# A new order for all engines in a fused attention and PReLU kernel, with alpha loaded in 16 rows

## The chip, the cores and the metric

One core of a Trainium2 chip runs the whole kernel. The metric is the device time of one execution in microseconds. A median over runs is compared, and one further execution was profiled.

## The reference

Eight batches, eight heads, 512 tokens and 32 states of width 64. Tokens attend to the states and the states to the tokens; both results, side by side, are the rows of a two-layer network.

```python
scores = scale * x @ state.T                  # per batch and head
a = softmax(scores);  xread = a @ state       # 512 rows of 64
a2 = softmax(scale * state @ x.T)
sread = a2 @ x                                # 32 rows of 64
rows = concat(xread, sread) over heads        # 8 * 544 = 4352 rows of 512
h = rows @ w_in                               # 512 -> 2048
g = maximum(h, 0) + alpha * minimum(h, 0)     # alpha: one value per column of h
out = g @ w_out                               # 2048 -> 512
```

## The kernel before

The kernel never forms xread. It multiplies the states with w_in first (`m`, 32 states of 4 heads in one PSUM bank, one `m` for each batch and each quarter f of w_in) and then the softmax weights with that product, so the first layer of a batch is 16 pairs of products (`F.b.jc`, two of 128x512). `f` is one half of such a pair, used for the first three of batch 0, where the weights of the first four heads are there before those of the others.

All work is one list of steps, `ORDER`, from which each engine gets its instructions in that order; there is no scheduler behind it, and waits come from the data and from the PSUM banks alone. A step's last numbers name the PSUM bank (0 to 5) or the engine: a is ScalarE (ACT), v is VectorE (DVE), p is GpSimd (POOL). A seventh place, the tile `two`, is shared by the scores of all batches and by those `m` that name no bank. The steps are:

- `lx0`, `lx`, `lst`, `wi`, `wo`: loads by GpSimd's DMA queue, which turns float32 into float16 on the way: x of a batch (batch 0 in two halves), the states, a quarter of w_in, a quarter of w_out.
- `stc`, `stt`, `sto`, `str`, `sro`: the states cast, transposed on TensorE and copied out.
- `xt`, `xo`: x of batches 0 and 1, transposed on TensorE and copied out. From batch 2 on, `xd` does it by a transposing DMA in SyncE's queue.
- `sc`: scores. `sb`, `smax`, `ssh`, `sexp`, `ssum`, `snorm`, `wb`: the softmax over the states (a 32x32 block transpose on VectorE, the maximum, the shift and the scaling on GpSimd, the exponential on ScalarE, and the transpose back). For batch 0 it is done in two halves, `.0` and `.1`; the state softmax of batch 0 reads `sc.0.0` and `sc.0.1`, the token softmax a second computation `sc.0`.
- `tm`, `te`, `tsum`, `tn`, `tt`, `rd`, `rdo`: the softmax over the tokens and the read of x with it.
- `m`, `mo`: states times w_in and its eviction, in two halves 0 and 1.
- `N`, `G`: on ScalarE `neg = relu(-h)`; on VectorE `g = neg * (1 - alpha) + h`. `oma` computes 1 - alpha.
- `S.b.q.jc2`, `O`: second layer, two products of 128x512 of the eight pairs that a block of 128 rows needs; then the eviction and store. `S` with jc2 of 6 and 7 reads the last quarter of w_out.
- `R`, `RO`, `L`, `LO`: the second layer of the 32-state rows, and the last block of rows in three pieces.
- `Z.k.n`: n products of zeros into bank k, whose results nobody reads.

Alpha (2048 values) is loaded by ScalarE's queue straight into the layout that `G` wants, value 128 jc + p in partition p, which makes each value a run of 4 bytes:

```python
alpha_sb = consts.tile([128, n_jc], F32)
nc.scalar.dma_start(alpha_sb, moe_alpha.rearrange("(jc p) -> p jc", p=128))
```

The order begins with the first batch's loads on GpSimd, then 20 zero products, the first states, 18 zero products, and the first two transposes of x:

```
stc lx0.0 lx0.1 oma id Z.1.20 stt.0 Z.2.18 xt.0.0.0.1 sto.a xt.0.1.0.2 xo.0.0.0.v lst xo.0.1.0.v
```

`xt.b.j.g` takes token half j of head group g; both transposes named here read the first half of batch 0's x, and `sc.0.0` needs both.

Of the kernel before, what the change touches and what calls it, by code (L numbers as in the profile page):

```python
# [28 lines left out]
N.0.9 G.0.6 S.0.1.2 smax.1 te.1.1 te.1.0 F.0.11.4 G.0.9 ssh.p.1 F.0.8.3 wo.3 N.0.8 N.0.11 S.0.0.3
S.0.1.3 m.0.3 G.0.8 F.0.10.0 mo.0.3.a.0 N.0.10 sexp.1 S.0.2.3 mo.0.3.v.1 xd.2 G.0.11 G.0.10  # L30
S.0.3.0.3 m.1.3 S.0.3.1 mo.1.3.a.0 F.0.14.4 S.0.2.4 F.0.13.0 N.0.14 tt.0 ssum.1 S.0.0.4 S.0.1.4
S.0.0.5 S.0.3.2 G.0.14 F.0.12.4 N.0.13 G.0.13 F.0.15.0 snorm.p.1 N.0.12 N.0.15 mo.1.3.a.1 wb.1
S.0.3.3 S.0.1.5 S.0.3.4 G.0.12 S.0.2.5 G.0.15 S.0.3.5 F.1.2.4 S.0.2.6 N.1.2 F.1.0.0 tsum.1 S.0.2.7
N.1.0 S.0.1.6 S.0.1.7 G.1.2 O.0.2.a sc.2 m.2.1.4.5 S.0.0.6 O.0.1.a F.1.7.2 mo.2.1.a.0 mo.2.1.a.1
G.1.0 F.1.1.0 tm.2 sb.2 F.1.3.4 N.1.7 S.0.0.7 S.0.3.6 N.1.1 G.1.1 N.1.3 tn.1.0 O.0.0.a te.2.0
F.1.5.5 S.0.3.7 N.1.5 G.1.3 F.1.9.0 S.1.1.0.1 G.1.7 F.1.4.4 smax.2 O.0.3.a S.1.1.1 tn.1.1 G.1.5
rd.0.2 te.2.1 N.1.9 G.1.9 m.2.3 F.1.6.3 N.1.4 rdo.0.a F.1.12.5 N.1.6 lx.3 G.1.4 F.1.13.2 N.1.12
F.1.8.0 G.1.6 G.1.12 S.1.2.0.4 N.1.13 G.1.13 ssh.p.2 N.1.8 S.1.1.2 F.1.11.3 G.1.8 F.1.10.5 N.1.11
S.1.2.1 N.1.10 G.1.11 G.1.10 S.1.2.2 sexp.2 S.1.1.3 ssum.2 F.1.14.2 F.1.15.0 snorm.p.2 mo.2.3.a.0
S.1.1.4 mo.2.3.a.1 S.1.1.5 m.3.2 m.4.2.3.5 N.1.14 tt.1 tsum.2 N.1.15 G.1.14 mo.3.2.a.1 S.1.1.6  # L40
S.1.2.3 S.1.2.4 mo.3.2.a.0 mo.4.2.a.0 G.1.15 mo.4.2.a.1 S.1.2.5 S.1.1.7 xd.3 O.1.1.a m.3.1.2.0
m.2.2.3.5 sc.3 wb.2 tn.2.1 S.1.2.6 S.1.2.7 mo.3.1.a.1 F.2.15.1 S.1.0.0.0 mo.2.2.a.0 mo.3.1.a.0
O.1.2.a lx.4 mo.2.2.a.1 sb.3 N.2.15 S.1.0.1 tm.3 F.2.13.3 N.2.13 G.2.15 S.1.0.2 F.2.4.2 tn.2.0
F.2.2.4 G.2.13 smax.3 N.2.4 F.2.9.5 F.2.0.1 N.2.9 S.1.0.3 S.1.0.4 G.2.9 S.1.0.5 N.2.2 N.2.0 te.3.0
F.2.12.3 S.1.0.6 N.2.12 G.2.2 G.2.4 G.2.0 xd.4 F.2.7.5 G.2.12 S.1.3.0.4 ssh.p.3 sexp.3 N.2.7 ssum.3
S.1.0.7 te.3.1 F.2.3.2 S.1.3.1 F.2.1.1 N.2.3 S.1.3.2 N.2.1 F.2.8.3 G.2.3 S.1.3.3 G.2.1 S.1.3.4
S.1.3.5 N.2.8 S.1.3.6 G.2.7 F.2.6.2 O.1.0.a N.2.6 m.3.3.1.0 G.2.8 sc.4 rd.1.5 snorm.p.3 F.2.5.3
G.2.6 mo.3.3.a.0 F.2.14.1 rdo.1.a wb.3 N.2.5 tsum.3 S.2.1.0.2 F.2.11.5 mo.3.3.a.1 G.2.5 S.1.3.7
N.2.14 F.2.10.0 F.3.4.3 G.2.14 N.2.11 S.2.1.1 F.3.1.1 lx.5 O.1.3.v N.3.4 S.2.1.2 N.2.10 G.2.11 tt.2
S.2.0.0.4 S.2.1.3 S.2.0.1 G.2.10 F.3.14.5 F.3.9.0 S.2.1.4 tn.3.1 N.3.1 N.3.9 G.3.1 S.2.1.5 S.2.0.2  # L50
G.3.4 tn.3.0 N.3.14 tm.4 F.3.3.1 F.3.8.3 G.3.14 N.3.8 G.3.9 S.2.1.6 S.2.1.7 S.2.0.3 S.2.3.0.5 N.3.3
xd.5 O.2.1.a tt.3 sb.4 G.3.8 smax.4 F.3.6.0 F.3.2.2 te.4.0 S.2.3.1 S.2.3.2 N.3.6 N.3.2 F.3.13.3
S.2.0.4 te.4.1 ssh.p.4 N.3.13 G.3.3 G.3.6 S.2.0.5 F.3.7.1 G.3.2 S.2.0.6 N.3.7 S.2.0.7 sexp.4 G.3.13
G.3.7 S.2.3.3 S.2.3.4 S.2.3.5 m.6.0 O.2.0.v m.5.1.0.2 mo.6.0.a.1 mo.5.1.a.1 rd.3.3 mo.6.0.v.0
rdo.3.a mo.5.1.v.0 rd.2.1 m.4.1.4.2 ssum.4 sc.5 m.4.3.0.3 rdo.2.a S.2.3.6 mo.4.1.a.1 mo.4.1.a.0 tm.5
tsum.4 snorm.p.4 F.3.5.1 mo.4.3.a.0 mo.4.3.a.1 F.3.0.2 F.3.10.4 N.3.0 S.2.3.7 O.2.3.a S.2.2.0.0
S.2.2.1 F.3.11.3 G.3.0 wb.4 S.2.2.2 S.3.3.0.5 F.3.15.2 S.3.3.1 N.3.5 lx.6 G.3.5 te.5.0 te.5.1 N.3.10
N.3.15 S.2.2.3 F.3.12.1 S.2.2.4 N.3.11 S.3.3.2 lx.7 N.3.12 G.3.10 G.3.15 F.4.6.4 N.4.6 tn.4.0
F.4.5.2 G.3.11 F.4.3.3 N.4.5 S.2.2.5 G.3.12 G.4.5 S.3.3.3 F.4.4.1 S.3.3.4 F.4.7.2 N.4.4 S.3.3.5
S.2.2.6 N.4.3 sb.5 N.4.7 S.3.3.6 S.2.2.7 G.4.4 G.4.7 S.3.3.7 F.4.1.1 F.4.0.2 xd.6 O.2.2.a S.3.1.0.0  # L60
O.3.3.a S.3.1.1 F.4.9.5 N.4.1 smax.5 G.4.6 N.4.0 S.3.0.0.4 tn.4.1 S.3.0.1 G.4.1 G.4.0 F.4.8.1
S.3.1.2 tsum.5 N.4.9 ssh.p.5 G.4.3 sexp.5 N.4.8 G.4.9 F.4.11.2 F.4.2.3 N.4.2 S.3.0.2 ssum.5 S.3.0.3
S.3.0.4 tt.4 N.4.11 S.3.1.3 G.4.8 S.3.1.4 S.3.1.5 G.4.2 S.3.1.6 snorm.p.5 m.5.0.5.1 G.4.11 sc.6
m.5.3.3.2 xd.7 wb.5 mo.5.0.a.1 sb.6 S.3.1.7 mo.5.3.a.0 mo.5.0.a.0 F.4.13.1 N.4.13 S.3.0.5 mo.5.3.a.1
S.3.2.0.3 tm.6 S.3.0.6 te.6.0 F.4.10.5 F.5.3.2 smax.6 S.3.2.1 N.4.10 N.5.3 S.3.2.2 S.3.2.3 S.3.0.7
S.3.2.4 S.3.2.5 S.3.2.6 ssh.p.6 G.4.13 O.3.1.a tn.5.0 F.4.14.1 te.6.1 O.3.0.v S.3.2.7 G.4.10 G.5.3
N.4.14 F.4.12.0 G.4.14 O.3.2.a sexp.6 tn.5.1 S.4.1.0.4 m.6.3 m.7.2.5.2 m.5.2.3.1 mo.6.3.v.0 S.4.1.1
mo.5.2.v.0 mo.7.2.a.0 S.4.1.2 mo.5.2.a.1 F.5.15.5 mo.6.3.v.1 mo.7.2.a.1 tt.5 S.4.1.3 N.5.15 G.5.15
F.4.15.3 F.5.12.1 S.4.1.4 F.5.5.2 N.4.12 F.5.13.5 S.4.1.5 N.5.12 N.4.15 G.4.12 tsum.6 G.4.15
S.4.0.0.0 S.4.1.6 S.4.1.7 N.5.5 S.4.0.1 S.4.2.0.3 O.4.1.v G.5.5 S.4.0.2 F.5.10.4 N.5.13 F.5.1.2  # L70
S.4.2.1 G.5.12 F.5.0.1 N.5.10 S.4.0.3 S.4.2.2 S.4.0.4 G.5.13 tn.6.1 N.5.0 G.5.10 N.5.1 G.5.1
m.6.1.5.4 m.7.0 mo.6.1.a.1 mo.6.1.a.0 S.4.0.5 mo.7.0.v.0 S.4.0.6 F.5.2.2 N.5.2 S.4.0.7 mo.7.0.v.1
G.5.0 O.4.0.a rd.4.4 rd.5.5 G.5.2 m.7.3.1.0 rdo.4.a m.6.2.2.4 sc.7 rdo.5.a ssum.6 mo.7.3.a.0
mo.6.2.a.0 snorm.p.6 tn.6.0 S.4.3.0.5 S.4.3.1 mo.7.3.v.1 F.5.11.1 S.4.3.2 sb.7 S.4.3.3 N.5.11 G.5.11
F.5.6.2 F.5.9.0 S.4.2.3 S.4.2.4 F.5.7.1 S.4.3.4 mo.6.2.a.1 F.5.8.4 smax.7 S.4.3.5 S.4.3.6 wb.6
S.4.3.7 S.4.2.5 N.5.9 N.5.8 N.5.7 G.5.9 O.4.3.a G.5.8 F.5.4.0 N.5.4 tt.6 S.5.0.0.4 S.5.2.0.5 S.4.2.6
G.5.7 G.5.4 F.5.14.1 S.5.2.1 tm.7 S.5.0.1 N.5.6 S.4.2.7 F.6.3.0 N.5.14 G.5.6 S.5.2.2 S.5.0.2 te.7.1
F.6.15.2 N.6.3 G.6.3 S.5.2.3 N.6.15 S.5.2.4 S.5.0.3 G.6.15 ssh.p.7 S.5.2.5 F.6.7.0 S.5.1.0.2 N.6.7
S.5.0.4 G.5.14 O.4.2.v S.5.1.1 F.6.6.1 G.6.7 F.6.8.3 te.7.0 S.5.1.2 N.6.6 S.5.1.3 sexp.7 F.6.1.0
tsum.7 N.6.8 N.6.1 G.6.6 S.5.2.6 F.6.0.1 S.5.0.5 tn.7.1 tn.7.0 S.5.0.6 G.6.8 S.5.2.7 F.6.10.3 tt.7  # L80
N.6.0 S.5.1.4 G.6.1 S.5.1.5 S.5.1.6 S.5.1.7 F.6.14.0 N.6.10 O.5.1.a ssum.7 G.6.10 S.5.0.7 F.6.5.3
snorm.p.7 F.6.2.2 N.6.14 N.6.5 G.6.0 S.5.3.0.1 O.5.0.v G.6.14 m.7.1 G.6.5 rd.7.4 rd.6.0 rdo.7.v
N.6.2 O.5.2.a F.6.13.3 S.5.3.1 mo.7.1.v.0 rdo.6.a S.5.3.2 S.5.3.3 mo.7.1.v.1 F.6.9.5 F.8.4.4 N.6.9
G.6.2 S.5.3.4 wb.7 F.6.12.0 G.6.9 F.6.4.2 N.6.13 N.6.12 S.5.3.5 G.6.12 N.6.4 S.5.3.6 S.5.3.7
S.6.0.0.5 S.6.0.1 N.8.4 F.6.11.0 G.6.13 G.6.4 F.8.10.3 N.6.11 S.6.0.2 N.8.10 O.5.3.v G.8.4 S.6.1.0.2
F.7.0.1 S.6.0.3 F.7.7.4 N.7.0 S.6.1.1 G.6.11 S.6.0.4 N.7.7 S.6.0.5 G.7.0 S.6.1.2 F.8.14.0 S.6.1.3
S.6.1.4 G.8.10 S.6.0.6 N.8.14 F.7.3.1 S.6.0.7 G.7.7 S.6.1.5 F.8.3.3 F.7.6.4 G.8.14 N.7.3 F.8.2.0
O.6.0.v G.7.3 F.7.2.5 F.8.9.1 S.6.1.6 N.8.3 G.8.3 S.6.2.0.3 N.8.2 N.7.2 S.6.2.1 G.8.2 S.6.2.2 N.7.6
# [547 lines left out]
```

## Time and profile before

| | |
|---|---|
| median of 3 runs | 218.97 us (218.73 to 219.55) |
| the profiled execution: time, span | 219.66 us, 217.9 us |
| TensorE busy in the span | 210.6 us (97%) |
| VectorE, ScalarE, GpSimd busy | 165.2, 137.4, 71.0 us |
| DMA | 23.12 MB, mean 106 GB/s |

Times in the profile's rows count from the span's start. A timeline row gives the start, the length, the engine (PE is TensorE, DVE VectorE, ACT ScalarE, POOL GpSimd, SP SyncE), the line, the operation, the output and the inputs by the program's names, and how many instructions are merged in it; in brackets stands how long the engine was idle before and what ended that. Products overlap in TensorE, so a merged row is longer than the distance to the next by the tail of its last product.

### The profile page before, as it was taken

How to read it: one execution, taken by the hardware profiler on the slowest of the kernel's cores; microseconds unless marked ns; L12 is line 12 of the kernel's file. 1: busy time of each engine (PE TensorE's matmuls, PEld its weight loads, DVE VectorE, ACT ScalarE, POOL GpSimd, SP SyncE). 2: the span in 40 equal slices, each digit the busy share in tenths (PEclk: the TensorE clock that was granted, in tenths of full speed). 3: DMA queues.
4: the chain of work that ended last, by engine and by line, in shares of the span. 5: the costliest groups of instructions: out<-in, count | busy, mean ns of one | idle time of the engine just before them, and what ended most of it. 6: DMA issues, size and time to landing. Idle time of an engine off the chain costs nothing.

```text
span 217.9 us, 4311 instructions
## 1 busy us (share of the span) xinstructions
PE 210.6 (97%) x1698; PEld 104.2 (48%) x1698; DVE 165.2 (76%) x250; ACT 137.4 (63%) x271; POOL 71.0 (33%) x58
## 2 busy tenths in 40 slices
...
GB/s 69 188 199 206 200 171 117 206 196 113 92 143 100 92 245 101 51 88 187 249 55 99 96 48 53 0 99 48 50 148 3 46 48 51 48 33 15 51 96 144
DMA packets 41748, 23.12 MB, mean 106 GB/s; under 512 B 24192, under 2 KB 38016, under 8 KB 41728
## 3 DMA queue, kind: packets, MB, share of 16 engines
...
q10 hardware_dynamic: 2064, 0.01, 0.5%
...
q14 instruction: 7, 0.06, 0.1%
...
## 4 chain that ended last, share of the span: by engine, by line
PE 84%; DMA 9%; DVE 3%; POOL 1%; issue 1%; ACT 0%; POOLq 0%
PE o L526 47%; PE h L474 23%; DMA xT<-xg 4%; DMA w_in_sb<-in_moe_w_in_dram 3%; PE m_ps L441 3%; PE h L483 3%; PE o L574 3%; DMA xg<-in_x_dram 2%; PE o L546 2%; PE sr_ps L416 2%; PE sc L291 1%; POOL an L352 1%; DVE ts L326 1%; DVE m L463 1%; DVE mx L332 1%
## 5 line engine op out<-in xcount | busy, mean ns | idle before, releaser
L526 PE MATMUL o<-w_out_sb,gt 128*128 128x512 f16 x496 | 125.3, 379 | 0.9 <-DMA w_out_sb<-in_moe_w_out_dram 0.9
L506 ACT ACTIVATE neg<-h 128x512 f32<-128x512 f32 (+1 forms) x144 | 77.1, 579 | 47.8 <-PE h L474 38.4
L514 DVE SCALAR_TENSOR_TENSOR gt<-neg,oma_sb,h 128x512 f16<-128x512 f32 x128 | 89.9, 738 | 16.5 <-ACT neg L506 15.6
L526 PEld LDWEIGHTS <-gt 128*128 128x128 f16 x496 | 47.3, 98 | 56.4 <-issue 4.5
L474 PE MATMUL h<-aT,m 128*128 128x512 f16 x250 | 68.3, 379 | 0.0
L474 PEld LDWEIGHTS <-m 128*128 128x128 f16 x250 | 24.1, 98 | 28.4 <-issue 0.6
L397 POOL TENSOR_SCALAR e<-e,r 128x512 f16<-128x512 f16 x16 | 25.0, 1566 | 20.4 <-DVE r L393 16.6
L463 ACT CAST m<-m_ps 128x512 f16<-128x512 f32 x50 | 27.1, 606 | 4.6 <-PE m_ps L441 4.3
L352 POOL TENSOR_TENSOR an<-ts,r 128x1024 f16<-128x1024 f32 (+1 forms) x9 | 15.4, 1719 | 33.2 <-DVE r L349 14.8
L338 POOL TENSOR_TENSOR ts<-ts,mx 128x1024 f32<-128x1024 f32 (+1 forms) x9 | 15.5, 1720 | 30.9 <-DVE mx L332 30.9
L564 ACT COPY osb<-o 128x512 f32<-128x512 f32 x22 | 12.9, 591 | 14.9 <-PE o L526 14.9
L441 PE MATMUL m_ps<-w_in_sb,stT 64*32 64x512 f16 x256 | 11.3, 383 | 0.6 <-DMA w_in_sb<-in_moe_w_in_dram 0.4
L383 ACT ACTIVATE e<-sc,nb 128x512 f16<-128x512 f32 x16 | 11.1, 700 | 1.1 <-DVE nb L375 1.1
L360 DVE STREAM_TRANSPOSE aT<-an 128x1024 f16<-128x1024 f16 (+1 forms) x9 | 10.1, 1120 | 1.9 <-POOL an L352 1.9
L514 DVE SCALAR_TENSOR_TENSOR gs<-neg,oma_sb,h 128x256 f16<-128x256 f32 x16 | 7.5, 476 | 4.5 <-ACT neg L506 4.5
L463 DVE CAST m<-m_ps 128x512 f16<-128x512 f32 x14 | 9.1, 679 | 2.0 <-ACT m L463 1.6
L372 DVE TENSOR_REDUCE nb<-sc 128x2 f32<-128x1024 f32 x8 | 9.6, 1202 | 0.5 <-PE sc L291 0.5
L332 DVE TENSOR_REDUCE mx<-ts 128x32 f32<-128x1024 f32 (+1 forms) x9 | 9.8, 1091 | 0.0
L348 DVE TENSOR_REDUCE r<-ts 128x32 f32<-128x1024 f32 (+1 forms) x9 | 9.8, 1087 | 0.0
L483 PE MATMUL h<-XS,w_in_sb 128*128 128x256 f16 x64 | 9.4, 273 | 0.0
L584 DVE COPY osr<-o 128x512 f32<-128x512 f32 x1 | 0.7, 692 | 11.3 <-PE o L574 11.3
L344 ACT ACTIVATE ts<-ts 128x1024 f32<-128x1024 f32 (+1 forms) x9 | 8.6, 960 | 0.2 <-POOL ts L338 0.2
...
## 6 DMA issues: line engine op xcount, KB each, us to landing
...
```

Source lines behind the costliest of these rows:

```text
L332: nc.vector.tensor_reduce(cols(live["mx", b], j, S // N), blocks(cols(live["ts", b], j, S)), AX.X, ALU.max)
L338: engine(e).tensor_tensor(ts, ts, over_blocks(cols(live["mx", b], j, S // N)), ALU.subtract)
L352: engine(e).tensor_tensor(blocks(cols(live["an", b], j, S)), blocks(cols(live["ts", b], j, S)), over_blocks(cols(live["r1", b], j, S // N) ...
L397: nc.gpsimd.tensor_scalar_mul(e2, e2, live["r2", b][:, g : g + 1])
L441: nc.tensor.matmul(t[N * k : N * (k + 1), :], st_head(b, h)[64 * r : 64 * r + 64, :], w_in_sb[64 * r : 64 * r + 64, c, 512 * f : 512 * (f ...
L463: copier(e)(m_tile(b)[:, f, g, :], live["mp", b, f][g])
L474: nc.tensor.matmul(h.rearrange("p (r j s) -> p r j s", r=2, j=2), ms[b][:, f, g, 128 * j : 128 * (j + 1)], weights(b, g), start=(g == 0), ...
L483: nc.tensor.matmul(h, w_in_sb[:, c, 128 * jc : 128 * (jc + 1)], XS[:, c].rearrange("p q n b -> p (q n b)"), start=(c == 0), stop=(c == n_c ...
L506: nc.scalar.activation(neg, h, RELU, bias=0.0, scale=-1.0)
L514: nc.vector.scalar_tensor_tensor(gt, negs.pop((b, jc)), oma_sb[:, jc : jc + 1], h, ALU.mult, ALU.add)
L526: nc.tensor.matmul(outs[b, q], gts[b, jc][:, 128 * q : 128 * (q + 1)], w_out_sb[:, jc, :], start=(jc == 0), stop=(jc == n_jc - 1),)
L564: copier(e)(osb, t)
```

## The change

`ORDER` is written anew. The last 166 of its 1055 steps keep their order, apart from PSUM banks; before them the steps are the same in kind and nearly in number, but stand in other places, and some evictions go from ScalarE to VectorE or back. The state shift of batch 7 and the scaling of batch 4 go from GpSimd to VectorE. The zero products are 74 in place of 82. The first eight of GpSimd's loads now stand ahead of its first softmax step: the first quarter of w_out and the third of w_in are moved there. The last quarter of w_out stands ahead of the state shift of batch 1.

Alpha is loaded as 16 rows of 128 values, into 16 of 32 partitions that are set to zero first, and VectorE transposes four 32x32 blocks before it computes 1 - alpha.

```diff
-stc lx0.0 lx0.1 oma id Z.1.20 stt.0 Z.2.18 xt.0.0.0.1 sto.a xt.0.1.0.2 xo.0.0.0.v lst xo.0.1.0.v
-Z.0.6 sc.0.0 xt.0.1.1.3 xt.0.0.1.4 sb.0.0 xo.0.0.1.v smax.0.0 xo.0.1.1.a str.0.5 sc.0.1 str.1.0 wi.0
-sro.0.a lx.1 wi.1 ssh.p.0.0 sb.0.1 Z.1.3 sc.0 Z.5.7 m.0.0.1.2 sro.1.a sexp.0.0 smax.0.1 m.3.0.3.4
-ssh.p.0.1 tm.0 mo.0.0.a.1 sexp.0.1 ssum.0.0 m.1.0.5.0 ssum.0.1 te.0.1 te.0.0 mo.1.0.v.1 wo.0
-mo.1.0.a.0 snorm.p.0.0 mo.3.0.a.1 Z.2.28 xt.1.1.1.2 xt.1.1.0.5 mo.0.0.a.0 snorm.p.0.1 wb.0.0
-mo.3.0.a.0 m.2.0 xt.1.0.1.0 xo.1.1.0.v xt.1.0.0.4 f.0.0.0.1 f.0.1.0.5 wi.2 mo.2.0.a.0 wb.0.1
-mo.2.0.a.1 f.0.1.1 xo.1.0.0.v N.0.1 m.0.1.3.4 f.0.0.1 mo.0.1.a.1 m.1.1 xo.1.1.1.v N.0.0 xo.1.0.1.v
-mo.0.1.v.0 f.0.2.0.2 F.0.3.0 f.0.2.1 F.0.4.3 mo.1.1.v.0 mo.1.1.a.1 F.0.7.4 G.0.1 N.0.2 G.0.0 wo.1
-F.0.5.5 N.0.3 G.0.2 wi.3 m.4.0 N.0.4 S.0.0.0.1 N.0.5 G.0.3 tsum.0 S.0.1.0.2 N.0.7 mo.4.0.a.1 G.0.4
...
+lx0.0 lx0.1 stc id Z.1.20 stt.0 lst wi.0 sto.v xt.0.1.0.1 Z.0.18 xt.0.0.0.2 xo.0.1.0.v xo.0.0.0.v
+Z.0.6 sc.0.0 xt.0.0.1.3 oma xo.0.0.1.a lx.1 wi.1 wo.0 sb.0.0 xt.0.1.1.4 xo.0.1.1.v str.0.5 sc.0.1
+sro.0.a smax.0.0 sb.0.1 str.1.0 smax.0.1 wi.2 sro.1.a ssh.p.0.0 Z.1.3 sc.0 ssh.p.0.1 Z.5.3 m.0.0.1.2
+tm.0 sexp.0.0 m.1.0.3.4 mo.0.0.a.0 ssum.0.0 sexp.0.1 m.2.0.5.0 ssum.0.1 mo.1.0.v.1 te.0.0 Z.1.24
+xt.1.1.1.1 mo.2.0.a.1 mo.2.0.a.0 xt.1.0.1.0 snorm.p.0.0 xt.1.0.0.5 wb.0.0 mo.0.0.a.1 snorm.p.0.1
+mo.1.0.a.0 xt.1.1.0.4 xo.1.0.1.a m.3.0.2.3 f.0.0.0.0 xo.1.1.1.v wb.0.1 te.0.1 f.0.1.0.1 wo.1 f.0.1.1
+mo.3.0.v.0 mo.3.0.a.1 wi.3 xo.1.0.0.v m.0.1 f.0.0.1 xo.1.1.0.v mo.0.1.v.1 f.0.2.0.2 m.1.1.3.5 N.0.1
+mo.0.1.a.0 F.0.3.4 G.0.1 f.0.2.1 tsum.0 N.0.0 mo.1.1.a.0 N.0.2 N.0.3 F.0.5.1 m.4.0 tn.0.1 F.0.4.3
+G.0.0 mo.1.1.v.1 tn.0.0 F.0.6.0 G.0.2 N.0.5 mo.4.0.a.0 wo.2 G.0.3 lx.2 N.0.4 S.0.0.0.5 S.0.1.0.2
...
-    alpha_sb = consts.tile([128, n_jc], F32)
-    nc.scalar.dma_start(alpha_sb, moe_alpha.rearrange("(jc p) -> p jc", p=128))
+    al32 = consts.tile([32, 128], F32)
+    nc.vector.memset(al32, 0.0)
+    nc.scalar.dma_start(al32[:n_jc, :], moe_alpha.rearrange("(jc p) -> jc p", p=128))
...
     def one_less_alpha():
-        nc.vector.tensor_scalar(oma_sb, alpha_sb, -1.0, 1.0, ALU.mult, ALU.add)
+        alT = consts.tile([128, 32], F32)
+        for k in range(4):
+            nc.vector.transpose(alT[32 * k : 32 * k + 32, :], al32[:, 32 * k : 32 * k + 32])
+        nc.vector.tensor_scalar(oma_sb, alT[:, :n_jc], -1.0, 1.0, ALU.mult, ALU.add)
```

More of the change, by code (lines that the diff above doesn't have):

```diff
@@ L29 @@
[L29 to L88, printed above, removed]
```

90 lines of the change are left out of this document (75 added, 15 removed).

## The prediction

> **What bounds the kernel now.** I read the page first (shares of the engines), then TensorE's busy time by stretches, then the chain of waits, and last the timelines of each engine up to 50 us.
>
> ```profile
> PE 210.6 (97%) x1698; PEld 104.2 (48%) x1698; DVE 165.2 (76%) x250; ACT 137.4 (63%) x271; POOL 71.0 (33%) x58
> ...
> 10.00:30.00 20.00, 18.92 (x226) 9.15 (x221) 19.13 (x34) 19.21 (x40) 13.80 (x14) 1.00 1.26 195
> ...
> 50.00:100.00 50.00, 49.86 (x422) 22.66 (x421) 46.63 (x67) 40.61 (x81) 22.55 (x15) 1.00 0.64 116
> 100.00:150.00 50.00, 50.00 (x381) 22.67 (x380) 43.39 (x61) 31.64 (x61) 15.72 (x9) 1.00 0.40 89
> ```
>
> The columns of a stretch are its length, the busy time of PE, PEld, DVE, ACT and POOL, the granted clock, the DMA share and GB/s. From 50 us on TensorE is never idle: 49.86 and 50.00 of 50 us. So the time is the moment at which TensorE becomes dense, plus the products left at that moment. Only what happens before can gain or lose, unless the new order opens a gap later. From 10 to 30 us DMA moves 195 GB/s without a pause, DVE is busy 19.13 and ACT 19.21 of 20 us: the head is bound by all of them together.
>
> The chain of waits (start, length, what) gives the head:
>
> ```profile
> 1.23 5.29 DMA xg<-in_x_dram
> 6.57 0.62 PE xT_ps L277 x4
> ...
> 15.75 7.17 DMA w_in_sb<-in_moe_w_in_dram
> ...
> 33.71 7.65 DMA xT<-xg
> ```
>
> The first half of batch 0 lands at 6.52; everything up to the softmax weights follows from it. At 33.71 SyncE starts the transposed load of batch 2, which lands at 41.36. TensorE's timeline (start, length, count in brackets as x; at the end the idle time before) shows what it did meanwhile:
>
> ```profile
> 0.98 2.31 PE L216 MATMUL z<-zero 128*128 128x128 f16 x20 [0.98 <-DVE zero L210]
> 3.59 0.42 PE L231 MATMUL st_ps<-ident,st 128*64 128x128 f16 x4 [0.30 <-POOL ident masks.py:199]
> 3.95 2.10 PE L216 MATMUL z<-zero 128*128 128x128 f16 x18
> 6.57 0.97 PE L277 MATMUL xT_ps<-ident,xg 128*128 128x128 f16 x8 [0.52 <-DMA xg<-in_x_dram]
> ...
> 8.05 0.30 PE L291 MATMUL sc<-xT,stT 64*32 64x256 f16 x8 [0.18 <-DVE xT L282]
> ...
> 12.78 1.72 PE L216 MATMUL z<-zero 128*128 128x128 f16 x28 [0.28 <-ACT m L463]
> ...
> 20.89 1.90 PE L526 MATMUL o<-w_out_sb,gt 128*128 128x512 f16 x8
> 22.96 0.41 PE L441 MATMUL m_ps<-w_in_sb,stT 64*32 64x512 f16 x8 [0.17 <-DMA w_in_sb<-in_moe_w_in_dram]
> ...
> 35.37 2.32 PE L526 MATMUL o<-w_out_sb,gt 128*128 128x512 f16 x10
> ...
> 38.97 0.59 PE L526 MATMUL o<-w_out_sb,gt 128*128 128x512 f16 x2 [0.85 <-DMA w_out_sb<-in_moe_w_out_dram]
> ...
> 41.41 0.41 PE L291 MATMUL sc<-xT,stT 64*32 64x256 f16 x16
> 41.63 0.40 PE L441 MATMUL m_ps<-w_in_sb,stT 64*32 64x512 f16 x8
> ```
>
> The second layer starts at 20.89. Three waits follow: 0.3 us for w_in at 22.96, 1.0 us for the last quarter of w_out at 38.97 (0.85 idle and the drained pipeline before it), 0.3 us for batch 2's transposed x at 41.41. Then none.
>
> **The measure.** The ten products from 35.37 take 2.32 us with a tail of 0.16, so 0.216 each. Nearly every step of the order (F and S are two such products, m is eight narrow ones, sc sixteen) costs TensorE about 0.43; I call that a block. Counted in the two orders from the first S: before, the first S that needs the last quarter of w_out is 39 blocks behind it and sc.2 is 44 behind; after, 37 and 42. Up to the first S both have done the same 37 steps in number and kind. Check of the measure: 20.89 + 44 x 0.43 + 0.3 + 1.0 + 0.3 = 41.4, which is where sc.2 stands.
>
> **Part 1, alpha.** The queue row of the old alpha load, and two stretches of the windows:
>
> ```profile
> q10 hardware_dynamic: 2064, 0.01, 0.5%
> ...
> 2.50:3.00 0.50, 0.50 (x8) 0.50 (x5) 0.00 (x0) 0.02 (x1) 0.50 (x2) 1.00 1.06 20
> 3.00:3.50 0.50, 0.29 (x3) 0.09 (x2) 0.23 (x1) 0.00 (x0) 0.42 (x3) 1.00 0.87 16
> ...
> 4.00:5.00 1.00, 1.00 (x12) 1.00 (x12) 0.17 (x1) 0.37 (x1) 1.00 (x3) 1.00 1.33 172
> ```
>
> 2064 packets for 8 KB fill the DMA engines from 2.5 to 3.5 us (share 1.06 and 0.87) while only 20 and 16 GB/s move. In 16 rows that is gone. Batch 0 then lands earlier by something between 0 (its own descriptors set its start) and 1.0 us (that whole stretch). I take 0.3, nearer to the lower end, because the load's issue on POOL ends only at 2.95 (row in part 4). So it lands at 6.2. The loads behind it run back to back, so all of them, the last quarter of w_out and batch 2 included, come about 0.3 earlier.
>
> The Trainium skill, "DMA: Bandwidth & Descriptors", section "Queues, rings and completion order", says that each DMA engine takes turns between its queues packet by packet; by it the tiny packets cost x turns only while both are queued, which again speaks for the small end. The sum would not go above 0.3 by it.
>
> VectorE turns alpha with four 32x32 transposes and the old scalar step. No row shows so small a transpose; bounds are 0.05 and 0.25 each, from the rows of 0.17 (128x16) and 0.72 (128x512 transpose) below. At 0.1 each that is 0.4 + 0.17 = 0.6 us, put between xo.0.0.0 and sb.0.0 on VectorE, where 0.45 us of waiting for sc.0.0 cover most of it: 0.1 left.
>
> **Part 2, the first transposes.** This is the costly one. Before, TensorE runs 18 zero products while it waits for x, then both transposes back to back. After, the first transpose (xt.0.1.0.1) stands ahead of those 18 zeros in TensorE's queue. TensorE therefore stands idle from 3.9 until x lands, and only then come 4 transposes, 18 zeros, 4 transposes, 6 zeros and sc.0.0. The zeros do no work, but the second transpose is queued behind them. VectorE's rows for what hangs on it:
>
> ```profile
> 4.06 0.17 DVE L248 TENSOR_SCALAR oma_sb<-alpha_sb 128x16 f32<-128x16 f32 x1 [0.69 <-DMA alpha_sb<-in_moe_alpha_dram]
> 7.21 0.78 DVE L282 COPY xT<-xT_ps 128x512 f16<-128x512 f16 x2 [2.98 <-PE xT_ps L277]
> 8.42 0.72 DVE L326 STREAM_TRANSPOSE ts<-sc 128x512 f32<-128x512 f32 x1 [0.42 <-PE sc L291]
> ...
> 9.96 0.70 DVE L326 STREAM_TRANSPOSE ts<-sc 128x512 f32<-128x512 f32 x1
> ...
> 15.88 0.70 DVE L360 STREAM_TRANSPOSE aT<-an 128x512 f16<-128x512 f16 x1
> ...
> 19.03 2.71 DVE L514 SCALAR_TENSOR_TENSOR gt<-neg,oma_sb,h 128x512 f16<-128x512 f32 x4
> ```
>
> After: x at 6.2; four transposes until 6.7; 18 zeros at the pace of the row at 3.95 (2.10 with its tail, 0.107 from one to the next) until 8.6; the second transpose's end at 9.25 (0.62 from the chain); its copy until 9.65 (half of 0.78); sc.0.0 at 9.7; the score transpose sb.0.0 0.4 later as before, 10.1 with the 0.1 of alpha nearly 10.2. Before it was 8.42: the head is 1.7 late.
>
> Here the clock matters. The zeros at 3.95 are 0.107 apart (2.10 for 18), those at 12.78 are 0.06 apart (1.72 for 28): TensorE was still slow after five microseconds of zeros. The Trainium skill, "TensorE: Matmul & The Clock Gate", section "What's actually happening", gives full clock only after some 3.4 us of sustained work. By it the 2.3 idle microseconds before x leave the array slow for all the zeros, as I assume; the rule speaks against this change. Were it full speed by 6.2, the zeros would take 18 x 0.06 = 1.1 and the head would be 0.8 less late (a rival below).
>
> **Part 3, from the scores to the first S.** VectorE's and POOL's steps are the same in kind. Ahead of sc.0.1 stand two x transposes and 14 state transposes, as before, but now at the slow clock, and its second input is copied by VectorE behind sb.0.0; so the second score transpose comes at 12.0 against 9.96: 2.0 late. The tail of the softmax keeps that: the last aT half at 17.8 against 15.88. Then ACT:
>
> ```profile
> 13.82 0.69 ACT L383 ACTIVATE e<-sc,nb 128x512 f16<-128x512 f32 x1
> ...
> 14.48 3.03 ACT L463 CAST m<-m_ps 128x512 f16<-128x512 f32 x6
> ...
> 19.63 2.56 ACT L506 ACTIVATE neg<-h 128x512 f32<-128x512 f32 x5
> ```
>
> te.0.1 (13.82 before) moves behind four evictions and a copy of 0.5 each; it ends near 19.1, and m.0.1 needs its PSUM tile, so TensorE waits there. N.0.1 follows at 19.6, and on VectorE (one eviction more and one copy less than before) G.0.1 at 20.4, G.0.0 at 21.2 (0.68 each by 2.71 for four), mo.1.1.v until 22.4. The first S needs that bank: about 22.9, against 20.89. sc.1 then waits for m.4.0's second eviction, fifth in ACT's list at 0.5 each: 0.45. The w_in wait of 0.3 goes, as TensorE comes later than the load.
>
> **Part 4, w_out and w_in issued earlier; softmax steps on VectorE.** POOL's rows (the first holds x's two issues, which end at 2.95):
>
> ```profile
> 1.23 1.72 POOL L178 DMA_DIRECT2D xg<-in_x_dram  x2 [0.80 <-POOLq L620]
> ...
> 10.12 1.05 POOL L338 TENSOR_TENSOR ts<-ts,mx 128x512 f32<-128x512 f32 x1 [3.67 <-DVE mx L332]
> ...
> 12.45 0.79 POOL L203 DMA_DIRECT2D w_out_sb<-in_moe_w_out_dram  x1
> ...
> L352 POOL TENSOR_TENSOR an<-ts,r 128x1024 f16<-128x1024 f32 (+1 forms) x9 | 15.4, 1719 | 33.2 <-DVE r L349 14.8
> ...
> L332 DVE TENSOR_REDUCE mx<-ts 128x32 f32<-128x1024 f32 (+1 forms) x9 | 9.8, 1091 | 0.0
> ```
>
> Two issues (0.8 us each) move ahead of POOL's first softmax step, into the 3.7 us that POOL idles there: free. They gain nothing: from 10 to 30 us the engines are never without work at 195 GB/s, so a longer queue only waits longer. The last w_out quarter stays behind batch 2's x and still collides with its transposed load. Behind the head, two softmax steps (snorm of batch 4, ssh of batch 7) go from POOL to VectorE, for which they cost between 1.1 (its own pass over as much) and 1.9 us (POOL's) each, and the evictions change hands one for one. I cost that at nothing: VectorE's idle 6.6 us between 100 and 150 hide it, and where they don't, it is rival 3.
>
> **Sum.** First S 22.9, plus 0.45, plus 42 blocks x 0.43 = 18.1: sc.2 at 41.4. The last w_out quarter is needed at 22.9 + 0.45 + 15.9 = 39.3, after its landing (38.9 less 0.3): its wait of 1.0 is gone. Batch 2's x lands at 41.36 less 0.3, so that wait goes too. But sc.2 stands where it stood, with two blocks fewer done: 2 x 0.43 = 0.86 late. I add 0.2 for gaps that the new order may open behind 41 us (before: none; bounds 0 and 3, nearest to none because the orders' distances between producer and user are alike). Total +1.1 us. The profiled execution has 217.9 us of span and 219.66 of time, 1.8 around it; it would become 219.0 and 220.8. The median of the runs, 218.97, is 0.7 below it, so I forecast 220.1. A measurement of this kernel can tell about 0.5% (1.1 us) from no change: the forecast is at that edge.
>
> **Rivals.**
> 1. *The head is shorter, DMA decides.* Clock full by 6.2, or x nearer to 5.6. Then TensorE reaches sc.2 early and waits for batch 2's x at 41.36 less 0.3 to 0.7, still two blocks short: +0.86 less 0.3 to 0.7, so +0.2 to +0.6: 219.4. For it: the wait of 0.3 at 41.41. Against: zeros at 0.107 after five microseconds. 0.24.
> 2. *Not slower: alpha's packets held up the whole stream.* If x lands by 5.2, 1.3 earlier, the 1.0 of lateness is undone; and if w_out's tail and the transposed load (7.65 in the chain) shift by as much or collide less, the 1.0 and 0.3 waits go as well: -0.5 to -1.5, so 218.0. It decides from a landing at 5.2 on. For it: 1.0 us of engines busy at under 20 GB/s. Against: POOL's issue ends at 2.95, and 256 KB at 172 GB/s take 1.5 more. 0.16.
> 3. *Late gaps.* An order planned for an earlier head runs VectorE and ACT (46.6 and 40.6 of 50 us busy) out of step; two or three waits of 0.5 to 1.0 behind 41 us: +2 to +3, so 221.5. For it: VectorE has only 3.4 us of slack in 50 to 100. Against: before shows no such wait. 0.20.
>
> **How the numbers follow.** The forecast has 0.40. Faster by over 0.5% (under 217.9): three quarters of rival 2, 0.12. Slower by over 0.5% (over 220.06): rival 3 and somewhat over two thirds of the forecast, 0.20 + 0.29 = 0.49. The rest, 0.39, is the same. The range reaches into rival 2 and rival 3 and leaves a tenth on either side: 218.0 to 221.9.
>
> **What would show it.** Right: idle TensorE from 3.9 to about 6.2; 18 zeros behind the first four transposes; sb.0.0 near 10.1; the first S near 22.9; no w_out wait near 39; no gap later. Wrong: the zeros at 0.06; x landing before 5.6; TensorE waiting at sc.2 for x; gaps behind 50 us; POOL's softmax late because eight loads in a row hold it up.

## The result, and the profile after

The changed kernel takes 220.76 us (median of 6 runs, 220.51 to 221.09) against 218.85 (6 runs on the same chip, 218.38 to 219.55): ratio 1.0082, 95% interval 1.0057 to 1.0107, so 1.9 us or 0.8% slower. The forecast was 220.1 and slower; the time is inside the range, 0.7 above the forecast. (Ratios, here and below, leave disturbed runs out and are not worked out from the two medians, so they need not equal their quotient.) The profiled execution took 220.85 us, with a span of 219.1.

Below, `sc.2` is the step with batch 2's first scores, the head is all work ahead of the second layer's first step, which is called the first S, and a late gap is a wait of TensorE behind `sc.2`. From the page after, the shares and the queue of alpha:

```profile
PE 212.3 (97%) x1690; PEld 104.2 (48%) x1690; DVE 167.9 (77%) x259; ACT 136.6 (62%) x269; POOL 67.9 (31%) x56
...
q10 hardware_dynamic: 32, 0.01, 0.0%
```

Alpha's 2064 packets are 32. The stretches behind the head, columns as before:

```profile
50.00:100.00 50.00, 49.97 (x465) 22.70 (x464) 46.98 (x67) 42.31 (x85) 22.35 (x14) 1.00 0.67 112
100.00:150.00 50.00, 49.91 (x372) 22.34 (x371) 45.41 (x66) 31.56 (x62) 17.84 (x11) 1.00 0.39 90
```

TensorE is still full from 50 us on, so the time is again decided ahead of that, but for 0.09 of idleness between 100 and 150 where before had none. TensorE's timeline after:

```profile
3.58 0.42 PE L232 MATMUL st_ps<-ident,st 128*64 128x128 f16 x4 [0.16 <-POOL ident masks.py:199]
5.23 0.61 PE L281 MATMUL xT_ps<-ident,xg 128*128 128x128 f16 x4 [1.22 <-DMA xg<-in_x_dram]
5.63 2.13 PE L217 MATMUL z<-zero 128*128 128x128 f16 x18
7.55 0.63 PE L281 MATMUL xT_ps<-ident,xg 128*128 128x128 f16 x4
7.98 0.85 PE L217 MATMUL z<-zero 128*128 128x128 f16 x6
8.76 0.41 PE L295 MATMUL sc<-xT,stT 64*32 64x256 f16 x8
...
22.43 1.71 PE L530 MATMUL o<-w_out_sb,gt 128*128 128x512 f16 x6
24.46 0.41 PE L295 MATMUL sc<-xT,stT 64*32 64x256 f16 x16 [0.33 <-ACT m L467]
...
41.40 0.41 PE L295 MATMUL sc<-xT,stT 64*32 64x256 f16 x16
```

The first half of batch 0's x landed at 5.18, 1.3 earlier than before. TensorE idled for it, transposed one part, and then did 18 zeros at 0.107 each (2.13 with the tail) with the second transpose queued behind them. The chain of waits names them as a link:

```profile
1.23 3.96 DMA xg<-in_x_dram
...
5.84 1.92 PE z L217 x18
```

VectorE's timeline over the same stretch:

```profile
8.22 0.43 DVE L286 COPY xT<-xT_ps 128x512 f16<-128x512 f16 x1 [1.92 <-PE xT_ps L281]
8.56 0.84 DVE L251 STREAM_TRANSPOSE alT<-al 32x32 f32<-32x32 f32 x4
9.44 0.18 DVE L252 TENSOR_SCALAR oma_sb<-alT 128x16 f32<-128x16 f32 x1
9.52 0.71 DVE L330 STREAM_TRANSPOSE ts<-sc 128x512 f32<-128x512 f32 x1
...
11.45 0.72 DVE L330 STREAM_TRANSPOSE ts<-sc 128x512 f32<-128x512 f32 x1 [0.25 <-PE sc L295]
...
17.33 0.71 DVE L364 STREAM_TRANSPOSE aT<-an 128x512 f16<-128x512 f16 x1
```

It waits 1.92 for the transpose behind the zeros. Thus x lands 1.3 earlier, and the score transpose sb.0.0 still comes 1.1 later than before (9.52 against 8.42).

**The bookkeeping.** sc.2 and what is left behind it make the span. In this profile sc.2 stands at 41.40 and 177.7 us follow. Of before, a second profile was taken later (label e8 below); there sc.2 stands at 40.26 and 176.5 follow. The difference of the two executions, 220.85 less 218.53 = 2.32 us, then divides so:

- First S: 22.43 against 20.94, +1.49.
- From the first S to sc.2: 42 blocks in 18.97 against 44 in 19.32, -0.35. At 0.43 a block that is 0.91 of waits against 0.40, +0.51, and two blocks fewer, -0.86.
- Behind sc.2: +1.18, of which the two blocks not yet done are +0.86, and 0.32 are late gaps.

The two blocks cancel. What is left is 1.49 of the head, and 0.51 and 0.32 of waits between engines later on. The largest late gap, on TensorE:

```profile
118.78 1.03 PE L530 MATMUL o<-w_out_sb,gt 128*128 128x512 f16 x4
119.90 0.59 PE L478 MATMUL h<-aT,m 128*128 128x512 f16 x2
```

Four products from 118.78 at 0.216 each would let the next start at 119.64; it starts at 119.90. What it waited for stands on ScalarE, in its timeline: three evictions of m, of which the second frees the PSUM bank that is needed here. The first of them waits for VectorE's eviction of the other half of the same m.

```profile
118.78 1.56 ACT L467 CAST m<-m_ps 128x512 f16<-128x512 f32 x3 [0.72 <-DVE m L467]
```

### The profile page after: what moved, and what is told of

It is laid out like the page before. It is cut to its first block, busy times and chain, and to the rows that moved or that the text cites. A ratio compares the mean times of both kernels' runs of the same rounds, so it can differ in the third digit from the quotient of the medians.

```text
span 219.1 us, 4300 instructions
## 1 busy us (share of the span) xinstructions
PE 212.3 (97%) x1690; PEld 104.2 (48%) x1690; DVE 167.9 (77%) x259; ACT 136.6 (62%) x269; POOL 67.9 (31%) x56
## 4 chain that ended last, share of the span: by engine, by line
PE 88%; DVE 5%; ACT 3%; DMA 2%; issue 1%; POOLq 0%
PE o L530 47%; PE h L478 24%; PE m_ps L445 3%; PE h L487 3%; PE o L578 3%; PE sr_ps L420 2%; DMA xg<-in_x_dram 2%; PE o L550 2%; DVE m L467 1%; ACT m L467 1%; PE sc L295 1%; PE z L217 1%; ACT neg L510 1%; PE xT_ps L281 1%; DVE gt L518 1%
## 5 line engine op out<-in xcount | busy, mean ns | idle before, releaser
L401 POOL TENSOR_SCALAR e<-e,r 128x512 f16<-128x512 f16 x16 | 25.7, 1611 | 27.1 <-DVE r L397 9.3
L342 POOL TENSOR_TENSOR ts<-ts,mx 128x1024 f32<-128x1024 f32 (+1 forms) x8 | 13.6, 1696 | 34.9 <-DVE mx L336 34.9
L356 POOL TENSOR_TENSOR an<-ts,r 128x1024 f16<-128x1024 f32 (+1 forms) x8 | 13.5, 1696 | 28.0 <-DVE r L353 28.0
L445 PE MATMUL m_ps<-w_in_sb,stT 64*32 64x512 f16 x256 | 12.3, 382 | 0.1
L467 DVE CAST m<-m_ps 128x512 f16<-128x512 f32 x15 | 10.0, 676 | 2.2 <-PE m_ps L445 1.3
L588 DVE COPY osr<-o 128x512 f32<-128x512 f32 x1 | 0.7, 692 | 11.3 <-PE o L578 11.3
L328 DVE STREAM_TRANSPOSE ts<-sc 128x1024 f32<-128x1024 f32 x7 | 8.7, 1244 | 0.3 <-PE sc L295 0.3
```

The lines of the kernel that those rows point to most:

```text
L342: engine(e).tensor_tensor(ts, ts, over_blocks(cols(live["mx", b], j, S // N)), ALU.subtract)
L356: engine(e).tensor_tensor(blocks(cols(live["an", b], j, S)), blocks(cols(live["ts", b], j, S)), over_blocks(cols(live["r1", b], j, S // N) ...
L401: nc.gpsimd.tensor_scalar_mul(e2, e2, live["r2", b][:, g : g + 1])
L445: nc.tensor.matmul(t[N * k : N * (k + 1), :], st_head(b, h)[64 * r : 64 * r + 64, :], w_in_sb[64 * r : 64 * r + 64, c, 512 * f : 512 * (f ...
L467: copier(e)(m_tile(b)[:, f, g, :], live["mp", b, f][g])
```

## The experiments

**e1: the zeros ahead of the first transpose.** The changed kernel with ten zeros in front of both transposes, as before's order has them, instead of 18 between them.

```diff
-... sto.v xt.0.1.0.1 Z.0.18 xt.0.0.0.2 xo.0.1.0.v xo.0.0.0.v
+... sto.v Z.2.10 xt.0.1.0.1 xt.0.0.0.2 xo.0.1.0.v xo.0.0.0.v
```

> The changed order, but the 18 zero products between the first two transposes of x are taken out, and 10 zero products (of a free bank) stand ahead of both transposes instead, so that TensorE is busy until about 5.0 us and then runs both back to back. Theory (the zeros behind the first transpose make the head late): batch 0's x lands near 5.2 as in the changed kernel, the first score transpose on VectorE moves from 9.5 to about 7.6 to 7.9, the first second-layer product from 22.4 to about 20.7, and TensorE then meets batch 2's transposed x (40.15 in the changed kernel) before it is there, so that sc.2 moves from 41.4 to 40.2: 1.2 us faster than the changed kernel, about 219.5. Rival (DVE and ACT set the head whatever the transposes do): first second-layer product stays within 0.5 us of 22.4 and the time within 0.4 us of the changed kernel's 220.8.

219.71 us (12 runs; ratio to before 1.0041, 1.0023 to 1.0059). TensorE's timeline of it:

```profile
5.46 1.03 PE L281 MATMUL xT_ps<-ident,xg 128*128 128x128 f16 x8 [0.26 <-DMA xg<-in_x_dram]
...
21.06 1.71 PE L530 MATMUL o<-w_out_sb,gt 128*128 128x512 f16 x6
23.09 0.41 PE L295 MATMUL sc<-xT,stT 64*32 64x256 f16 x16 [0.33 <-ACT m L467]
...
40.03 0.41 PE L295 MATMUL sc<-xT,stT 64*32 64x256 f16 x16
```

First S 1.37 earlier than in the changed kernel, sc.2 too, and the time 1.05 shorter by the medians, 0.9 by the ratios to before. So the place of the zeros costs about 1 of the 1.9 us. TensorE did not meet batch 2's x too early, as had been expected: it had landed at 39.50. The other two terms stay: sc.1 still waits 0.33 for ScalarE's eviction, and 177.92 follow sc.2.

**e2: alpha's rows alone.** Before, with alpha in 16 rows and its four transposes.

```diff
-    alpha_sb = consts.tile([128, n_jc], F32)
-    nc.scalar.dma_start(alpha_sb, moe_alpha.rearrange("(jc p) -> p jc", p=128))
+    al32 = consts.tile([32, 128], F32)
+    nc.vector.memset(al32, 0.0)
+    nc.scalar.dma_start(al32[:n_jc, :], moe_alpha.rearrange("(jc p) -> jc p", p=128))
...
```

> The kernel before with alpha in 16 rows and its four transposes on VectorE, and nothing else. Theory: x of batch 0 lands at 5.2 in place of 6.5; the 18 zeros of the old order end near 5.8, so the transposes start there, 0.8 earlier; the stream of loads is at most 0.3 earlier, so the waits for w_out (38.97) and for batch 2's x (41.41) stay and most of the 0.8 is given back: 0 to 0.5 us faster than before. Rival (the packets of alpha held up the whole head and the loads): 1.0 us faster or more, with the last quarter of w_out landing a full microsecond earlier.

219.06 us (12 runs; 1.0021, 0.9998 to 1.0044): no gain, though x landed at 5.43 against 6.26 to 6.52 in the three profiles of before and e5, and the score transpose came at 7.53 against 7.92 to 8.42. TensorE's timeline of it shows where that stayed in the profiled execution:

```profile
14.86 0.62 PE L281 MATMUL xT_ps<-ident,xg 128*128 128x128 f16 x8 [1.02 <-DMA xg<-in_x_dram]
...
39.59 0.59 PE L530 MATMUL o<-w_out_sb,gt 128*128 128x512 f16 x2 [1.68 <-DMA w_out_sb<-in_moe_w_out_dram]
```

It waited for batch 1's x, and then for the last quarter of w_out. The loads behind the first one did not come earlier with it. This execution, of 220.09 us, lies 1.0 above the median of its twelve, so the size of these waits need not be that of a typical run.

**e3: the changed kernel with the old alpha.**

```diff
-    al32 = consts.tile([32, 128], F32)
-    nc.vector.memset(al32, 0.0)
-    nc.scalar.dma_start(al32[:n_jc, :], moe_alpha.rearrange("(jc p) -> jc p", p=128))
+    alpha_sb = consts.tile([128, n_jc], F32)
+    nc.scalar.dma_start(alpha_sb, moe_alpha.rearrange("(jc p) -> p jc", p=128))
...
```

> The changed order with the old load of alpha in 4-byte runs and without the transposes on VectorE. Theory: x lands at 6.5 in place of 5.2 and the head, which nothing covers in this order, is later by as much: first second-layer product near 23.5, time 1.0 to 1.3 us above the changed kernel, about 221.9. Rival (DMA of w_out and of batch 2's x decides, the head is covered): within 0.4 us of the changed kernel.

220.98 us (6 runs; 1.0107, 1.0080 to 1.0134). Its profile, an execution of 221.73 us, is the expected one: x at 6.44, first S at 23.30, sc.2 at 42.28, each 0.9 to 1.3 later. The median is only 0.2 above the changed kernel's (0.5 by the ratios to before), so the expectation on the time missed, and the rival's "within 0.4" holds by the medians. The profiled execution lies 0.75 above the median; the new alpha is worth between 0.2 and 0.9 in this order.

**e4: the loads back.** The changed kernel with w_out's first quarter and w_in's third behind GpSimd's first softmax steps again, and the other quarters of w_out, the last one above all, back in their old places.

```diff
-... xo.0.0.1.a lx.1 wi.1 wo.0 sb.0.0 ... smax.0.1 wi.2 sro.1.a ssh.p.0.0 Z.1.3 sc.0 ssh.p.0.1 Z.5.3 ...
+... xo.0.0.1.a lx.1 wi.1 sb.0.0 ... smax.0.1 sro.1.a ssh.p.0.0 Z.1.3 sc.0 ssh.p.0.1 wo.0 Z.5.3 ...
```

> The changed kernel, but the loads of w_out (four quarters) and the third quarter of w_in stand in GpSimd's list where the kernel before has them: behind the softmax steps. Theory (the loads queue in the DMA engines, their issue time does not matter): landings within 0.3 us, time within 0.4 us of the changed kernel, unless the last quarter, issued behind the state shift of batch 1, now collides more with the transposed load of batch 2 (it landed at 38.9 before, 36.4 in the changed kernel): then up to 0.5 slower. Rival (moving the loads forward is worth something): 0.7 us slower or more.

220.83 us (6 runs; 1.0095, 1.0069 to 1.0121), as the changed kernel. The first quarter of w_out landed at 21.12 instead of 19.77 and the last at 37.92 instead of 36.41, and sc.2 stood at 41.45 instead of 41.40. The expectation on the time held, that on the landings (within 0.3 us) did not: the move does bring these loads forward, by 1.4 and 1.5 us. TensorE waits for them in neither profile.

**e5: before, with the last quarter of w_out ahead of batch 2's x.**

```diff
-... S.0.2.1 lx.2 sb.1 ... F.0.8.3 wo.3 N.0.8
+... S.0.2.1 wo.3 lx.2 sb.1 ... F.0.8.3 N.0.8
```

> The kernel before, but GpSimd issues the last quarter of w_out ahead of batch 2's x, so that the transposed load of batch 2, which starts when x has landed, cannot run into it any more. Theory (the 1.0 us wait for w_out in the profiled execution of before comes from that collision, and its size is chance): no wait for w_out near 39, last quarter landed by about 34; batch 2's x lands near 36 and its transposed form near 40.3, so that sc.2 stands at 40.3 to 40.8; span near 217, and times close to the fast end of before's runs (218.2 to 218.6) with little spread. Rival (the wait in the profile is there in every run): the median falls by 0.7 us or more below before's 218.7.

218.93 us (12 runs; 1.0013, 0.9997 to 1.0030). The quarter landed at 34.03 and the wait for it is gone, but batch 2's x comes later and its transposed copy bounds sc.2, by TensorE's timeline:

```profile
40.76 0.41 PE L291 MATMUL sc<-xT,stT 64*32 64x256 f16 x16 [0.25 <-DMA xT<-xg]
```

That is 0.65 earlier than in the first profile of before. Had the waits of that profile been there in every execution, this gain would have shown in the median; it did not. The small spread that was expected did not come either: eleven of the twelve runs lie between 218.51 and 220.29.

**e8: before once more**, unchanged, for a second profile.

> The kernel before once more, unchanged but for a comment, for a second profile. Theory (the wait for w_out is chance): the profile has another wait for w_out than 1.0 us, and span minus that wait stays at 216.7 to 217.0; behind sc.2 the same 176.47 us to the end. Rival: wait and span as in the first profile.

Profiled at 218.53 us, 1.1 less than the execution that the prediction's sum was made against. Its TensorE timeline at the place of the waits:

```profile
38.01 0.59 PE L526 MATMUL o<-w_out_sb,gt 128*128 128x512 f16 x2
...
38.87 1.46 PE L526 MATMUL o<-w_out_sb,gt 128*128 128x512 f16 x6
40.26 0.41 PE L291 MATMUL sc<-xT,stT 64*32 64x256 f16 x16
```

No wait for w_out (landed at 37.46, not 38.93), none for batch 2 (40.06, not 41.36). So the waits of the first profile, 1.3 us together, are not there in every execution. The last quarter of w_out and the transposing load are under way at the same time in both, and how late they land differs between the two. This execution is the fastest of its eight, 0.4 below their median, so a typical run may still pay some 0.4 of it.

**e6: e1 with sc.1 one step later**, so that ScalarE's eviction is there when TensorE comes.

```diff
-G.0.5 mo.4.0.a.1 S.0.1.1 sc.1 m.0.2.4.1 ... G.0.4 S.0.0.1 S.0.2.0.3
+G.0.5 mo.4.0.a.1 S.0.1.1 S.0.0.1 sc.1 m.0.2.4.1 ... G.0.4 S.0.2.0.3
```

> The variant of the changed kernel with ten zero products ahead of the first transposes, and in addition the step S.0.0.1 ahead of sc.1, where TensorE waited 0.5 us for an eviction on ScalarE. Theory (part 3's second wait is TensorE's and is covered by a block that is ready): sc.2 moves from 40.03 to about 39.6, where batch 2's transposed x (39.5) takes over; 0.4 us faster than that variant, about 219.3. Rival (VectorE's prelu steps set the pace there): no change within 0.2 us.

219.66 us (10 runs; 1.0033, 1.0014 to 1.0052), as e1, which is the rival's number. The wait at sc.1 is gone and the stretch from the first S to sc.2 is 18.78 instead of 18.97, but in the profiled execution, of 220.22 us, the head was held elsewhere:

```profile
15.72 1.07 PE L281 MATMUL xT_ps<-ident,xg 128*128 128x128 f16 x16 [1.73 <-DMA xg<-in_x_dram]
```

Batch 1's x landed at 15.67 there, against 14.17 in e1. So the price of the wait at sc.1 stays open: at most 0.4, and not seen in the median.

**e7: three parts that looked free, together on before**: alpha's rows, ten zeros instead of 18 ahead of the transposes, w_out's last quarter ahead.

> The order of the kernel before with three edits: alpha in 16 rows, 10 in place of 18 zero products ahead of the first transposes, and the last quarter of w_out ahead of batch 2's x. Theory: head 1.3 us earlier (first second-layer product near 19.8 to 20.2), then the wait for the third quarter of w_in near 22.5 and batch 2's transposed x near 40 decide: sc.2 near 40.0 to 40.3, span 216.6, time 218.2 to 218.5, 0.3 us below before. Rival (DVE and ACT give the head away): same as the run with the w_out edit alone.

219.08 us (12 runs; 1.0007, 0.9989 to 1.0025): as before and as e5, so the rival. By its TensorE timeline the scores begin at 6.72, 1.3 and 0.8 us before those of the two profiles of before (8.05, 7.55), and nothing is left of it at sc.2:

```profile
6.72 0.30 PE L295 MATMUL sc<-xT,stT 64*32 64x256 f16 x8 [0.29 <-DVE xT L286]
...
15.34 0.62 PE L281 MATMUL xT_ps<-ident,xg 128*128 128x128 f16 x8 [1.11 <-DMA xg<-in_x_dram]
...
40.94 0.41 PE L295 MATMUL sc<-xT,stT 64*32 64x256 f16 x16 [0.51 <-DMA xT<-xg]
```

Batch 1's x, landed at 15.29, and batch 2's transposed x, landed at 40.89, hold it. In before's order an earlier head was worth nothing in e2 and e7, whose loads did not come earlier with it.

**e9: the zeros alone.** Before, its old alpha and all else kept, with the 18 zeros moved behind the first transpose.

```diff
-... stt.0 Z.2.18 xt.0.0.0.1 sto.a xt.0.1.0.2
+... stt.0 xt.0.0.0.1 Z.2.18 sto.a xt.0.1.0.2
```

> The kernel before with one part of the change alone: the 18 zero products that stood ahead of the first x transpose stand behind it, between the first two transposes; everything else, the old alpha and the place of the loads included, is as before. Theory (the place of the zeros is the cause of the lateness): the first score product comes at 10.0 to 10.5 us instead of 7.9 to 8.4, the first S product at 22.3 to 23.0 instead of 20.9, and as TensorE waits for the last quarter of w_out or for batch 2's transposed x in before at most about 1 us, sc.2 comes at 41.2 to 42.0 instead of 40.3; the rest behind sc.2 stays 176.5, and the time is 0.9 to 1.6 us above before, 219.8 to 220.5. Rival (the DMA sets sc.2 in before's order and covers a later head): sc.2 stays within 0.4 us of before's 40.3 to 41.4 and the time within 0.4 us of before, at most 219.3.

220.64 us (12 runs; 1.0062, 1.0034 to 1.0091) against 218.99: 1.4 us by the ratio, within what the theory had. One step in the list makes before as slow as the changed kernel, and the waits that before has anyway do not cover it. TensorE's timeline of its profile:

```profile
5.81 0.61 PE L277 MATMUL xT_ps<-ident,xg 128*128 128x128 f16 x4 [1.81 <-DMA xg<-in_x_dram]
6.21 2.13 PE L216 MATMUL z<-zero 128*128 128x128 f16 x18
...
9.49 0.30 PE L291 MATMUL sc<-xT,stT 64*32 64x256 f16 x8
...
21.95 1.90 PE L526 MATMUL o<-w_out_sb,gt 128*128 128x512 f16 x8
```

The first S is 1.0 behind e8's, less than the 1.4 to 2.1 expected, and the scores come at 9.49, ahead of the 10.0 to 10.5 expected: x landed 0.5 earlier, for which the edit gives no reason. This execution, of 222.07 us the longest of the twelve, then also waited 1.0 for w_in and 1.5 for w_out, so its sc.2 at 43.82 does not price the zeros. It does show a second way by which they may cost time in before's order: GpSimd issues the loads behind its softmax steps there, w_out's first quarter at 13.89 against 12.19 in e8. How much of the 1.4 us goes that way was not tried; in the changed kernel the first eight loads stand ahead of those steps.

**e10: e7 with sc.2 four blocks later**, the one version from which a gain over before was hoped.

```diff
-O.0.2.a sc.2 m.2.1.4.5 ... G.1.0 F.1.1.0 tm.2 sb.2
+O.0.2.a m.2.1.4.5 ... G.1.0 F.1.1.0 sc.2 tm.2 sb.2
```

> The kernel before with alpha in 16 rows, 10 zeros instead of 18 ahead of the first transpose and the last quarter of w_out loaded ahead of batch 2's x (the run that did these three alone), and with batch 2's first score products (sc.2) four blocks later, so that they find batch 2's transposed x landed. Theory (only the wait at sc.2 holds the earlier head back): no wait at sc.2, and the time is 0.4 to 0.6 us below that run, about 218.5, 0.2 to 0.4 below before. Rival (the earlier head is held back at batch 1's x, or the later sc.2 comes back as a wait behind it): within 0.2 us of that run, 218.9 to 219.3.

220.05 us (12 runs; 1.0031, 0.9999 to 1.0062): above e7 by 1.0 in the medians and by 0.5 in the ratios to before. The theory had it 0.4 to 0.6 below, the rival within 0.2; the rival's reason is what the profile shows, at a higher price. The wait at sc.2 is gone and a longer one stands behind it. On TensorE and on VectorE:

```profile
41.62 0.41 PE L295 MATMUL sc<-xT,stT 64*32 64x256 f16 x16
...
45.36 0.61 PE L478 MATMUL h<-aT,m 128*128 128x512 f16 x2 [1.07 <-DVE gt L518]
```

```profile
42.10 1.22 DVE L376 TENSOR_REDUCE nb<-sc 128x2 f32<-128x1024 f32 x1 [2.03 <-PE sc L295]
...
43.44 1.24 DVE L328 STREAM_TRANSPOSE ts<-sc 128x1024 f32<-128x1024 f32 x1
44.60 2.02 DVE L518 SCALAR_TENSOR_TENSOR gt<-neg,oma_sb,h 128x512 f16<-128x512 f32 x3
```

VectorE's list has tm.2 and sb.2 ahead of the next G. It stands idle for 2.03 until the scores are there, does the two, and only then frees the PSUM bank that the next F needs. No version that was run beats before.

## Why the prediction was right, and where it was off

- **What bounds it** held. TensorE is full behind the head in both. What follows sc.2 is 176.46 to 176.50 in every profile of before's order that leaves the steps behind it alone, and 177.68 to 177.92 in every one of the new order, whatever the head did. The count of two blocks (0.86) is the larger part of that 1.2, and the new order has saved the same 0.86 ahead of sc.2.
- **Part 1, alpha**, was off twice. x came 1.3 earlier than with the old alpha in the new order (after against e3) and 1.1 in the old one (e2 against before); over all profiles the medians are 5.43 (seven, 5.18 to 5.85) and 6.28 (five, 5.76 to 6.52). That is 0.85 to 1.3, not 0.3, on either side of the upper bound of 1.0. The argument for the small end, that GpSimd's issue ends at 2.95 anyway, fails: the issue stands at 1.23 with a length of 1.72 in the changed kernel too, yet x lands at 5.18. With alpha in 32 packets the loads are under way half a microsecond sooner. After, by the windows:

```profile
3.00:3.50 0.50, 0.42 (x4) 0.28 (x3) 0.01 (x1) 0.00 (x0) 0.42 (x3) 1.00 0.68 81
3.50:4.00 0.50, 0.42 (x4) 0.18 (x3) 0.00 (x0) 0.00 (x0) 0.50 (x2) 1.00 1.41 190
```

Before, the same half microseconds moved 16 and 98 GB/s; by the packets' own times in that trace, alpha's ran from 2.1 to 3.5. The transposes took 0.84 together, not 0.4, and with sc.0.0's end at 9.17 they hold sb.0.0 back by 0.35, not 0.1. The rule quoted from the Trainium skill, "DMA: Bandwidth & Descriptors", section "Queues, rings and completion order", was read as speaking for the small end; the measured difference speaks against that reading. The step "all loads behind it come 0.3 earlier" has no support: batch 1's x landed between 13.90 and 14.89 in the five profiles with the old alpha and between 13.95 and 15.67 in the seven with the new.
- **Part 2, the zeros**, was right and the main cause: e1 takes about 1 us back by it, e9 brings on 1.4 with it alone. From x's landing to sb.0.0 it forecast 3.9; it was 4.34 (9.52 less 5.18), 1.90 before. The zeros ran at 0.107 as assumed, with the full clock granted only from 11.3 on; the idle stretch ahead of x was 1.2, not 2.3, as x came earlier.
- **Part 3**: three of its times came about half a microsecond below their forecast, as x was 1.0 earlier and the way from x to sb.0.0 0.44 longer than assumed, 0.25 of it by alpha's steps: second score transpose 11.45 (12.0), last aT half 17.33 (17.8), first S 22.43 (22.9). The step ahead of the first S did not: VectorE waited 0.43 for ScalarE's `neg`, and mo.1.1.v ended at 22.37, as forecast (22.4). The first S followed it by 0.06, where the prediction had left 0.5 without a reason. So it is by that allowance that the first S is half a microsecond early. The wait at sc.1 was 0.41 (0.45); two further waits of 0.2 each, for VectorE's G.0.2 behind 22.65 and for another G behind 33.53, were not foreseen.
- **Part 4**: the loads are worth nothing (e4), though not because the queue was never empty: put back, the same loads landed 1.4 later. They are worth nothing because TensorE comes later still. The two softmax steps took 1.2 us each on VectorE, inside their bounds, and are hidden.
- **The sum**: sc.2 at 41.4 as forecast, 41.40, from errors that cancel (head 0.5 earlier, waits 0.5 longer). The allowance for late gaps was 0.2 and is 0.32.
- **The mis-sized term** is the credit for waits that go. The sum set 1.3 us of waiting for w_out and batch 2 against the later head, as if before paid it every time. e8 shows before without it, and e5 takes the w_out wait away for no gain. That is why the forecast of +1.1 became +1.9: credited with the 0.4 that a typical run may pay, an estimate from the median of e8 and its profiled execution, it would have been +2.0. Against the first profile the forecast was exact (220.8 and 220.85); that the median of before lay 0.7 below that execution was taken off both sides, though it was the sign that its waits are not typical.
- **Rivals.** Rival 2's condition came true (x at 5.18, which is also one of the prediction's own signs of being wrong) without its result: the head swallowed it, and e2 shows that before's order would have gained nothing either. Rival 1 would have needed the head of e1, whose time, 219.7, is near its 219.4. Rival 3's mechanism is there at about a tenth of its size.

What stays open is how the remaining 0.9 us (by the ratio of e1) between e1 and before divide in the median. Profile against profile (219.72 and 218.53) they are head +0.12, waits up to sc.2 +0.51 and late gaps +0.56; e6 could not confirm the second.
